# Scores and state sums of 128-token chunks in halves of 64 tokens, on quarters of the TensorE array

## Chip, cores, metric

The kernel runs on one core of a Trainium2 chip. The metric is the device time of one execution in microseconds (us); lower is better. A changed kernel is timed against the kernel before, and for this kernel a difference of 0.2% (2 us) is about what can be told from none.

## What is computed

Three layers follow each other: a gated linear attention and two feed-forward layers. Inputs are float32, but the weights come as float64 and are split on the chip into a high and a low part.

```python
# attention: 4 batches, 8 heads, 768 tokens, head size 48
for t in range(S):
    state = alpha[:, :, t, :, None] * state + np.einsum('bhd,bhe->bhde', k[:, :, t], v[:, :, t])
    y[:, :, t] = np.einsum('bhd,bhde->bhe', q[:, :, t], state)
x = y.transpose(0, 2, 1, 3).reshape(3072, 384)
x = ((x @ w_a) * (x @ w_b)) @ w_out                                   # 384 -> 1536 -> 384
h = x @ w_in                                                          # 384 -> 2048
return (np.maximum(h, 0.0) + alpha2 * np.minimum(h, 0.0)) @ w_out2    # 2048 -> 384
```

## The kernel before

The tokens are worked on in six blocks of 512: block n holds 128 consecutive tokens of each of the four batches. One batch's 128 tokens are a chunk, so a block is four chunks (`BC`), and there are 24. The state of a batch, `Z[:, c]`, passes from its chunk in one block to its chunk in the next. The eight heads lie as four pairs j, a pair's head i on partitions 64*i to 64*i+47.

A chunk (function `chunk`, from L353) does this. VectorE (DVE) forms the running products of alpha by two scans (L401, L411) and multiplies k and q by them (L416), so that inside the chunk plain matmuls do. TensorE (PE) transposes k (`pe_k`, tile kps, L452), and ScalarE (ACT) copies it out to `ks` (L456). PE forms the scores `A` of all 128 x 128 token pairs of each head (`pe_a`, L470: 48 rows deep, 128 columns out, 128 tokens streamed; the two heads of a pair in the two row halves of the array). DVE multiplies them by the causal mask into `As` (`ev_a`, L479). PE forms the chunk's own state sum `dS` from ks and v (`pe_d`, L503), and the result `y`: v against the masked scores (`intra`, L521, 128 rows deep) plus the old state against q (`inter`, L527, 48 by 48, four matmuls in the four quarters of the array at once). DVE then adds dS to Z (`kept`, L582), ACT and DVE split y into a high and a low part (L605, L609) for the feed-forward matmuls. All of these matmuls are float32; in the trace each leaves two MATMUL and two LDWEIGHTS records.

Block 0 starts from no state (`start`); block 1 (`moved`) packs its heads into 384 rows by three shift matmuls (`pe_m`, L563) and so does y in two parts; the last block (`end`) needs no dS.

The feed-forward layers are groups of nine matmuls of 128 x 512: `pa`, `pb` and `acc` of the first layer, `pi` and `acc` of the second (`mm3`, L641 to L644). Its DVE work is the product (L771) and the low part (L668).

The order on each engine is fixed when the program is built. A planner (`Graph.run`) gives every operation a duration (the numbers in `A("PE", 1200, ...)`), a key (its due time) and dependencies, and takes, engine by engine, the ready operation of the smallest key. A chunk's operations are due some 9.5 us apart ahead of their block, and lie between feed-forward groups. Where the planner leaves PE idle early in the program, `fill` puts matmuls on constants there (`wp`, L184), for 0.7 of the idle time. PSUM: the scores `A` and the result `y` use one tile of two banks in turn (tag `pair`, ring `pring`); kps and dS use a third bank in turn (tag `att`).

Of the kernel before, what the change touches and what calls it, by code (L numbers as in the profile page):

```python
# [21 lines left out]
P = 128  # L22
CH = 128
BC = 4
# [114 lines left out]
def body(tc, akq, v, vg, w_a, w_b, w_o1, w_in, w_o2, beta, out):  # L139
# [13 lines left out]
    with ExitStack() as ctx:  # L153
# [199 lines left out]
        def chunk(g):  # L353
# [118 lines left out]

            def ev_a(h):
                def f():
                    if 0 in h:
                        s["As"] = tp.tile([P, 2, NJ, CH], F32, name="As", tag="As", bufs=1)
                    m = mask.rearrange("p (o t) -> p o t", o=1).to_broadcast([P, len(h) * NJ, CH])
                    flat = lambda x: x.rearrange("p i j t -> p (i j) t")
                    nc.vector.tensor_tensor(out=flat(s["As"][:, h[0] : h[-1] + 1]),  # L479
                                            in0=s["A"][h[0]] if start else flat(s["A"]), in1=m, op=ALU.mult)  # L480
                return f

            w = sring.take()
            if start:
                (b0, w0, h0), (b1, w1, h1) = bank(1), bank(2)
                abanks = (b0, b1)
                pa = A("PE", 1200, pe_a, [k1, q1, *w0, *w1])
                a0 = A("DVE", 660, ev_a([0]), [pa, *w])
                a1 = A("DVE", 660, ev_a([1]), [pa, a0])
# [7 lines left out]
            if ks is not None:  # L497
                def pe_d():
                    s["dS"] = dbank("dS")[:, :, 0:D]
                    for j in range(NJ):  # L500
                        for i in range(2):
                            hs = slice(64 * i, 64 * i + 64)
                            nc.tensor.matmul(s["dS"][hs, j, :], s["ks"][:, j, hs],  # L503
                                             s["v"][:, 2 * j + i, 0:D], start=True, stop=True)
# [7 lines left out]

            def y_of(j, rows=slice(0, P)):
                return s["y"][rows, j % 2, j // 2, :]

            def intra(j, first, last):
                for i in range(2):
                    o = 64 * (i ^ (j & 1))  # L520
                    nc.tensor.matmul(y_of(j, slice(o, o + 64)), s["v"][:, 2 * j + i, :],  # L521
                                     s["As"][:, i, j, :], start=first, stop=last)

            def inter(j, last):
                for i in range(2):
                    ps, o = slice(64 * i, 64 * i + D), 64 * (i ^ (j & 1))
                    nc.tensor.matmul(y_of(j, slice(o, o + D)), Z[ps, c, j, :], qT()[ps, j, :],  # L527
                                     start=False, stop=last)

            def pe_y():  # L530
                s["y"] = two_banks("y")
                if start:

                    for j in range(KT):
                        intra(j, j < 2, False)
                    for j in range(KT):
                        for i in range(2):
                            nc.tensor.matmul(y_of(j, slice(64 * i, 64 * i + 64)), s["vg"][:, j, i, :],
                                             s["As"][:, i ^ (KT & 1), KT, :], start=False, stop=j > 0)
                    return  # L540
                if moved:
                    intra(KT, True, False)
                    inter(KT, True)
                    return
                for j in range(NJ):
                    intra(j, j < 2, False)
                for j in range(NJ):
                    inter(j, j > 1)

            py = A("PE", 1600 if start else 600 if moved else 1600, pe_y, [a0, a1, lv, q1, zs, *pring.take()])  # L550
            yhold = pring.last()
            if moved:
# [4 lines left out]
                def pe_m():  # L557
                    for j in range(KT):
                        intra(j, j < 2, False)
                    for j in range(KT):  # L560
                        inter(j, False)
                    for j in range(KT):
# [13 lines left out]
            if not end:  # L576
                def kept():
# [17 lines left out]
            def two(part):  # L595

                x = xt[n][:, part, :, cols].rearrange("p (k b) t -> p b k t", b=2)
                y = s["y"][:, :, 0 : NJ // 2, :]
                return [(x, y)] if nt == NJ else [(x[:, :, 0], y[:, :, 0]), (x[:, 0, 1], y[:, 0, 1])]
# [30 lines left out]

        for g in range(NG):
            chunk(g)
# [274 lines left out]
def layout(q, k, v, alpha, moe_w_a, moe_w_b, moe_w_out, moe2_w_in, moe2_w_out, moe2_alpha):  # L907
# [6 lines left out]
    def padded(x, fill):  # L914
# [14 lines left out]
    swap = lambda x, j: x[::-1] if j & 1 else x  # L929
    vg[..., D:] = (  # L930
        swap(v[:, H - 2 :, :CH].swapaxes(0, 1), KT).reshape(2, B, CH, KT, GR).transpose(1, 2, 3, 0, 4)
    )
# [3 lines left out]
        np.concatenate([np.arange(D) + (2 * t + i) * D, np.arange(GR) + (2 * KT + k) * D + GR * t])  # L936
        for t in range(KT) for i, k in zip(swap((0, 1), t), swap((0, 1), KT))
# [27 lines left out]
```

## Time and profile before

| what | us |
|---|---|
| timed runs | 976.03 to 976.87, median 976.53 |
| profiled execution: span from first to last instruction | 974.6 |
| its own time beside the span | not given; the median of the timed runs lies 1.9 above the span |
| PE busy | 962.7 (99%) |
| DVE busy | 607.0 (62%) |
| ACT busy | 252.3 (26%) |

The span is what the sums of the prediction are made against, and 1.9 us are added for the time around it. A PE that is shown busy is not a PE at its peak: the records overlap, and how long a piece of work holds PE is read from the starts of what follows.

### The profile page before, as it was taken

The page shows a single profiled execution, that of the slowest core. Times are in us where ns is not written, and L with a number is a line of the kernel's source. Part 1 is how long each engine was busy: PE and PEld are TensorE (multiplying, and loading weights), DVE is VectorE, ACT ScalarE, POOL GpSimd, SP SyncE. Part 2 cuts the span into 40 slices and gives each one's busy share as a digit, 9 for nine tenths or more (in the row PEclk, how much of TensorE's full clock was granted, in tenths as well). Part 3 has the DMA queues.
Part 4 walks back from the last instruction along what each step waited for, and adds up shares of the span by engine and source line. Part 5 has one row for each costly group of instructions (what it writes and reads, how often), then busy time and mean ns, then how long its engine had stood idle before and what let it go on. Part 6 is the DMA issues. An engine that isn't in the chain of part 4 may idle for free.

```text
span 974.6 us, 12831 instructions
## 1 busy us (share of the span) xinstructions
PE 962.7 (99%) x5330; PEld 777.9 (80%) x5330; DVE 607.0 (62%) x867; ACT 252.3 (26%) x417; POOL 4.5 (0%) x18
## 2 busy tenths in 40 slices
PE   6999999999999999999999999999999999999998
PEld 5777888778877887887788888888888888888886
DVE  8989888667678868876322254554555545545554
ACT  2444443232333333242121121111111111111111
POOL 1000000000000000000000000000000000000000
PEclk9999999999999999999999999999999999999999
DMA  8962000133457535652055550020100200200000
GB/s 324 405 245 76 1 12 1 55 119 126 170 197 233 199 119 203 193 199 99 33 186 201 193 192 22 1 98 1 65 33 1 86 11 1 98 1 1 32 1 33
DMA packets 31066, 103.92 MB, mean 107 GB/s; under 512 B 3488, under 2 KB 4256, under 8 KB 31008
## 3 DMA queue, kind: packets, MB, share of 16 engines
q1 hardware_dynamic: 30864, 102.97, 29.5%
q8 instruction: 42, 0.69, 0.3%
q10 hardware_dynamic: 144, 0.13, 0.0%
q14 instruction: 16, 0.13, 0.0%
HBM read 74.78 MB, written 26.74 MB: 104 GB/s over the span
## 4 chain that ended last, share of the span: by engine, by line
PE 99%; DVE 0%; DMA 0%; issue 0%; ACT 0%; DVEq 0%; ACTq 0%
PE acc L641 12%; PE acc L644 12%; PE acc L642 12%; PE pi L641 7%; PE pi L642 7%; PE pi L644 7%; PE pa L641 5%; PE pb L641 5%; PE pa L642 5%; PE pb L642 5%; PE pb L644 5%; PE pa L644 5%; PE A L470 3%; PE y L521 2%; PE y L527 1%; PE dS L503 1%
## 5 line engine op out<-in xcount | busy, mean ns | idle before, releaser
L664 ACT CAST gh<-ng 128x512 fp32r<-128x512 f32 x96 | 59.5, 620 | 327.8 <-DVE ng L877 271.2
L873 DVE TENSOR_SCALAR ng<-pi,betaT 128x512 f32<-128x512 f32 x96 | 72.1, 751 | 106.5 <-PE pi L644 105.5
L771 DVE TENSOR_TENSOR a_sb<-a_sb,pb 128x512 f32<-128x512 f32 x72 | 49.5, 688 | 108.4 <-PE pb L644 108.4
L668 DVE TENSOR_TENSOR gl<-ng,gh 128x512 fp32r<-128x512 f32 x96 | 66.3, 691 | 80.0 <-ACT gh L664 79.9
L641 PE MATMUL acc<-gh,v 128*128 128x512 f32 x288 | 113.4, 394 | 0.0
L641 PE MATMUL pi<-x,v 128*128 128x512 f32 x288 | 113.3, 393 | 0.0
L642 PE MATMUL pi<-x,v 128*128 128x512 f32 x288 | 112.7, 391 | 0.0
L644 PE MATMUL acc<-gl,v 128*128 128x512 f32 x288 | 112.7, 391 | 0.0
L642 PE MATMUL acc<-gh,v 128*128 128x512 f32 x288 | 112.0, 389 | 0.0
L641 PE MATMUL acc<-gh,wo 128*128 128x512 f32 x216 | 86.7, 401 | 0.0
L641 PE MATMUL pa<-x,wa 128*128 128x512 f32 x216 | 86.3, 400 | 0.0
L641 PE MATMUL pb<-x,wb 128*128 128x512 f32 x216 | 86.1, 399 | 0.0
L644 PE MATMUL acc<-gl,wo 128*128 128x512 f32 x216 | 84.8, 392 | 0.0
L642 PE MATMUL pa<-x,wa 128*128 128x512 f32 x216 | 84.6, 392 | 0.0
L642 PE MATMUL pb<-x,wb 128*128 128x512 f32 x216 | 84.6, 392 | 0.0
L642 PE MATMUL acc<-gh,wo 128*128 128x512 f32 x216 | 84.1, 390 | 0.0
L768 ACT COPY a_sb<-pa 128x512 f32<-128x512 f32 x72 | 42.3, 588 | 155.4 <-PE pa L644 155.4
L644 PE MATMUL pi<-x,v 128*128 128x512 f32 x288 | 81.6, 391 | 0.0
L664 ACT CAST gh<-a_sb 128x512 fp32r<-128x512 f32 x72 | 44.8, 622 | 126.7 <-DVE a_sb L771 120.8
L877 DVE SCALAR_TENSOR_TENSOR ng<-pi,ng 128x512 f32<-128x512 f32 x96 | 66.4, 691 | 3.1
L641 PEld LDWEIGHTS pi<-x,v 128*128 128x128 f32 x288 | 54.1, 188 | 13.7 <-DVE ng L877 2.1
L644 PEld LDWEIGHTS acc<-gl,v 128*128 128x128 f32 x288 | 54.1, 188 | 12.6
(109 smaller groups left out, 1430.8 us busy)
## 6 DMA issues: line engine op xcount, KB each, us to landing
kq<-in_akq SPq DMA_DIRECT2D x24, 512.0 KB, 4.5
w2d<-ws SPq DMA_DIRECT2D x16, 768.0 KB, 3.7
v<-w2d SPq DMA_DIRECT2D x16, 768.0 KB, 5.5
x2d<-x SPq DMA_DIRECT2D x18, 512.0 KB, 3.7
x<-x2d SPq DMA_DIRECT2D x6, 1536.0 KB, 6.9
ra<-in_akq SPq DMA_DIRECT2D x24, 258.5 KB, 3.4
v<-in_v SPq DMA_DIRECT2D x24, 256.0 KB, 4.9
rs<-in_w_in SPq DMA_DIRECT2D x8, 768.0 KB, 6.0
```

The lines of the kernel that those rows point to most:

```text
L470: nc.tensor.matmul(A[i][:, j, :], kT()[ps, j, :], qT()[ps, j, :], start=True, stop=True)
L503: nc.tensor.matmul(s["dS"][hs, j, :], s["ks"][:, j, hs], s["v"][:, 2 * j + i, 0:D], start=True, stop=True)
L521: nc.tensor.matmul(y_of(j, slice(o, o + 64)), s["v"][:, 2 * j + i, :], s["As"][:, i, j, :], start=first, stop=last)
L641: nc.tensor.matmul(o, lh, rh, start=first and n == 0, stop=False)
L642: nc.tensor.matmul(o, ll, rh, start=False, stop=False)
L644: nc.tensor.matmul(o, lh, rl, start=False, stop=last and n == len(pairs) - 1)
L664: nc.scalar.copy(gq[idx][0], src())
L668: nc.vector.tensor_tensor(out=gl, in0=src(), in1=gh.bitcast(F32), op=ALU.subtract)
L768: nc.scalar.copy(b["a"], ba["t"])
L771: nc.vector.tensor_tensor(out=b["a"], in0=b["a"], in1=bb["t"], op=ALU.mult)
L873: nc.vector.tensor_scalar(out=b["n"], in0=bh["t"], scalar1=0.0, scalar2=betaT[:, i : i + 1], op0=ALU.min, op1=ALU.mult)
L877: nc.vector.scalar_tensor_tensor(out=b["n"], in0=bh["t"], scalar=0.0, in1=b["n"], op0=ALU.max, op1=ALU.add)
```

## The change

In all blocks but the first, a chunk's 128 tokens are taken as two halves h of 64. Scores are formed only inside a half (`A` is 64 by 64, 16 matmuls for 8, in the four quarters of the array), and the mask is 64 by 64 for both halves, so DVE's masking has 512 elements a partition for 1024. What the first half gives to the second goes by the state: the state sum is formed for each half (16 matmuls for 8, 64 rows deep), a new DVE operation `mid` adds the first half's sum to Z and gives `z1`, and the second half's `inter` uses z1. `pe_d` and `pe_y` become `pe_cross` (half of the intra matmuls, and both state sums) and, behind `mid`, `pe_own` (the other half of intra, and inter in 16 matmuls for 8). dS no longer has a bank of its own in these blocks: it lies in the free part of y's two banks, which are therefore also held until `mid` and `kept` have read them. The last block now transposes k too and forms the first half's sum. In block 1 the y of the shifted heads is no longer made in two parts: `pe_m` holds the three shift matmuls alone. Once, ACT copies a quarter of the mask (`halve`). The heads take other slots in y, and the rows of w_a and w_b are permuted to suit when the inputs are laid out. Block 0 keeps its matmuls.

```diff
--- before.py
+++ after.py
...
-            if not end:
+            if not (start and end):
                 def pe_k():
...
             def pe_a():
-                s["A"] = [b(f"A{i}") for i, b in enumerate(abanks)] if start else two_banks("A")
-                A = s["A"] if start else [s["A"][:, i] for i in range(2)]
+                if start:
+                    s["A"] = [b(f"A{i}") for i, b in enumerate(abanks)]
+                    for j in range(NJ):
+                        for i in range(2):
+                            ps = slice(64 * i, 64 * i + D)
+                            nc.tensor.matmul(s["A"][i][:, j, :], kT()[ps, j, :], qT()[ps, j, :],
+                                             start=True, stop=True)
+                    return
+                s["A"] = two_banks("A").rearrange("p i j t -> p i (j t)")[:, :, 0 : NJ * HC]
+                A = s["A"].rearrange("p i (j t) -> p i j t", t=HC)
                 for j in range(NJ):
-                    for i in range(2):
-                        ps = slice(64 * i, 64 * i + D)
-                        nc.tensor.matmul(A[i][:, j, :], kT()[ps, j, :], qT()[ps, j, :],
-                                         start=True, stop=True)
-
-            def ev_a(h):
+                    for h in range(2):
+                        hs = slice(h * HC, (h + 1) * HC)
+                        for i in range(2):
+                            ps = slice(64 * i, 64 * i + D)
+                            nc.tensor.matmul(A[hs, i, j, :], kT()[ps, j, hs], qT()[ps, j, hs],
+                                             start=True, stop=True)
+
...
+                    m = mask[:, 0:HC].rearrange("p (a o t) -> p a o t", a=1, o=1).to_broadcast([P, 2, NJ, HC])
+                    a = s["A"].rearrange("p i (j t) -> p i j t", t=HC)
+                    nc.vector.tensor_tensor(out=s["As"], in0=a, in1=m, op=ALU.mult)
...
-                pa = A("PE", 1200, pe_a, [k1, q1, *pring.take()])
-                a0 = a1 = A("DVE", 1200, ev_a([0, 1]), [pa, *w], 0, slack)
+                pa = A("PE", 600, pe_a, [k1, q1, *pring.take()])
+                a0 = a1 = A("DVE", 700, ev_a(0), [pa, halved[0], *w], 0, slack)
...
+            def slot_of_head(j, i):
+                return 2 * i + j // 2, j % 2
+
+            def y_of(k, rows=slice(0, P), t=slice(0, CH)):
+                return s["y"][rows, k // 2, k % 2, t]
...
-            py = A("PE", 1600 if start else 600 if moved else 1600, pe_y, [a0, a1, lv, q1, zs, *pring.take()])
...
+                part_of = lambda h: slice(h * HC, (h + 1) * HC)
+                def intra(j, i, h, first):
+                    k, p = slot_of_head(j, i)
+                    nc.tensor.matmul(y_of(k, half(p), part_of(h)), s["v"][part_of(h), 2 * j + i, :],
+                                     s["As"][part_of(h), i, j, :], start=first, stop=False,
+                                     skip_group_check=True)
+                def inter(j, i, h, z, last):
+                    k, p = slot_of_head(j, i)
+                    ps = slice(64 * i, 64 * i + D)
+                    nc.tensor.matmul(y_of(k, slice(64 * p, 64 * p + D), part_of(h)), z[ps, j, :],
+                                     qT()[ps, j, part_of(h)], start=False, stop=last,
+                                     skip_group_check=True)
+                def pe_cross():
+                    s["y"] = two_banks("y")
+                    flat = s["y"].rearrange("p i j t -> p i (j t)")
+                    s["dS"] = [flat[:, 1 - h, 2 * CH : 2 * CH + NJ * D].rearrange("p (j d) -> p j d", d=D)
+                               for h in range(2)]
+                    for j in range(NJ):
+                        for h in range(2):
+                            intra(j, 1 - h, h, j < 2)
+                    for j in range(NJ):
                         for i in range(2):
+                            for h in range(1 if end else 2):
+                                nc.tensor.matmul(s["dS"][h][half(i), j, :], s["ks"][part_of(h), j, half(i)],
+                                                 s["v"][part_of(h), 2 * j + i, 0:D], start=False,
+                                                 stop=j == NJ - 1, skip_group_check=True)
+                def mid():
+                    s["z1"] = s["At"][:, NJ * CH : NJ * CH + NJ * D].rearrange("p (j d) -> p j d", d=D)
+                    nc.vector.tensor_tensor(out=s["z1"], in0=s["dS"][0], in1=Z[:, c, :, :], op=ALU.add)
+                def pe_own():
+                    for j in range(NJ):
+                        for i in range(2):
+                            intra(j, i, i, False)
+                    for h, z in ((0, Z[:, c]), (1, s["z1"])):
+                        for j in range(NJ):
+                            for i in range(2):
+                                inter(j, i, h, z, h == 1 and j > 1)
+                pc = A("PE", 850, pe_cross, [a0, ks, lv, *pring.take()])
+                yhold = pring.last()
+                kring.use(pc)
+                z1 = A("DVE", 360, mid, [pc, zs])
+                py = A("PE", 850, pe_own, [z1, zs, q1])
+                yhold.append(z1)
...
                 def pe_m():
-                    for j in range(KT):
-                        intra(j, j < 2, False)
-                    for j in range(KT):
-                        inter(j, False)
-                    for j in range(KT):
-                        nc.tensor.matmul(y_of(j), shift[:, j, :], s["y3"], start=False, stop=j > 0)
-
+                    for k in range(KT):
+                        nc.tensor.matmul(y_of(k), shift[:, k, :], s["y3"], start=False, stop=k > 0,
+                                         skip_group_check=True)
+
+                lhold.append(py)
                 x = A("ACT", 280, ev_3, [py, *yring.take()])
-                py = A("PE", 2200, pe_m, [x])
+                py = A("PE", 750, pe_m, [x])
...
-                        nc.vector.tensor_tensor(out=z, in0=s["dS"], in1=z, op=ALU.add)
-
-                x = A("ACT" if start else "DVE", 360, kept, [ds] if start else [ds, zs, py])
-                dhold.append(x)
+                        nc.vector.tensor_tensor(out=z, in0=s["dS"][1], in1=s["z1"], op=ALU.add)
+
+                x = A("ACT" if start else "DVE", 360, kept, [ds] if start else [z1, py])
+                (dhold if start else yhold).append(x)
+                if not start:
+                    sring.use(x)
...
+                def halve():
+                    nc.scalar.copy(mask[HC:, 0:HC], mask[HC:, HC:])
+                halved.append(G.add("ACT", 250, halve, block_at[1] - 60000, masked))
...
```

The planner lays the engines' orders out anew. On PE, around the fourth chunk of block 2, these rows stand before (a row is a line, an operation, out<-in and its shape; pa is a feed-forward group):

```order
L452 MATMUL kps<-plus,kq 128x128 x4
L470 MATMUL A<-kq 128x128 x8
L503 MATMUL dS<-v,ks 64x48 x8
L641 MATMUL pa<-x,wa_1500 128x512
L642 MATMUL pa<-x,wa_1500 128x512
L641 MATMUL pa<-x,wa_1500 128x512
L642 MATMUL pa<-x,wa_1500 128x512
L641 MATMUL pa<-x,wa_1500 128x512
L642 MATMUL pa<-x,wa_1500 128x512
L644 MATMUL pa<-x,wa_1500 128x512 x3
L521 MATMUL y<-As,v 64x128 x8
L527 MATMUL y<-kq,Z 48x128 x8
```

After the change the same chunk's `pe_cross` (first two rows) and `pe_own` (last three rows; `y<-kq,As` is the inter on z1, which lies in As's tile) stand like this, and its A stands two groups earlier, by itself:

```order
L558 MATMUL y<-As,v 64x64 x8
L581 MATMUL y<-v,ks 64x48 x16
L699 MATMUL pb<-x,wb_1747 128x512
L700 MATMUL pb<-x,wb_1747 128x512
L699 MATMUL pb<-x,wb_1747 128x512
L700 MATMUL pb<-x,wb_1747 128x512
L699 MATMUL pb<-x,wb_1747 128x512
L700 MATMUL pb<-x,wb_1747 128x512
L702 MATMUL pb<-x,wb_1747 128x512 x3
L558 MATMUL y<-As,v 64x64 x8
L565 MATMUL y<-kq,Z 48x64 x8
L565 MATMUL y<-kq,As 48x64 x8
```

What moved: the attention interrupts the feed-forward groups three times for this chunk (A, cross, own) instead of twice, with one group of nine between cross and own; so it is in all 16 chunks of blocks 2 to 5, but for block 2's first, where two groups stand there.

On DVE the rows around that chunk's `mid` (L587) are, after the change:

```order
L829 TENSOR_TENSOR a_sb<-a_sb,pb 128x512
L496 TENSOR_TENSOR As<-A,mask 128x512
L791 TENSOR_TENSOR x_2336<-part_1169,x_2336 128x512
L726 TENSOR_TENSOR gl<-a_sb,gh 128x512
L417 TENSOR_TENSOR kq<-kq,ra 128x1024
L587 TENSOR_TENSOR As<-y,Z 128x192
L408 RECIPROCAL invs<-ra 128x4
L431 TENSOR_TENSOR Z<-Z,ra 128x192
L412 SCALAR_TENSOR_TENSOR ra<-ra,invs 128x516
L829 TENSOR_TENSOR a_sb<-a_sb,pb 128x512
L632 TENSOR_TENSOR Z<-y,As 128x192
```

Before, a chunk's y waited for no sum of its dS on DVE; now `pe_own` waits for `mid`, which stands behind the next chunk's product of k and q (L417) here, and `kept` (L632) follows behind the next product of the feed-forward. In the whole order there are 125 `wp` matmuls where there were 84; all 41 new ones lie among block 1's chunks.

## Rows read from the trace of the kernel before

**Rows 1.** The page, its first line.

```profile
span 974.6 us, 12831 instructions
```

**Rows 2.** Busy time by engine (x records) in three stretches: block 1's chunks, feed-forward only, block 2's chunks.

```profile
core 0: us, PE busy (x) PEld busy (x) DVE busy (x) ACT busy (x) POOL busy (x), PEclk, DMA share, GB/s
36.00:48.00 12.00, 12.00 (x85) 8.61 (x81) 10.94 (x19) 4.96 (x11) 0.00 (x0) 1.00 1.03 411
100.00:170.00 70.00, 70.00 (x307) 57.45 (x306) 61.98 (x87) 30.71 (x45) 0.00 (x0) 1.00 0.02 5
170.00:225.00 55.00, 55.00 (x439) 43.36 (x439) 38.63 (x56) 13.49 (x23) 0.00 (x0) 1.00 0.34 109
```

**Rows 3.** Timeline of PE (start, length, line, out<-in, records), block 2's first chunk.

```profile
175.09 0.60 PE L452 MATMUL kps<-plus,kq 128*128 128x128 f32 x4
...
176.71 0.50 PE L641 MATMUL pb<-x,wb 128*128 128x512 f32 x1
177.05 0.40 PE L642 MATMUL pb<-x,wb 128*128 128x512 f32 x1
...
178.21 0.85 PE L644 MATMUL pb<-x,wb 128*128 128x512 f32 x3
...
179.93 0.40 PE L642 MATMUL acc<-gh,wo 128*128 128x512 f32 x1
```

**Rows 4.** Timeline of PE, block 3's second chunk.

```profile
278.48 0.60 PE L452 MATMUL kps<-plus,kq 128*128 128x128 f32 x4
279.01 1.16 PE L470 MATMUL A<-kq 48*128 48x128 f32 x16
...
281.05 0.39 PE L642 MATMUL acc<-gh,wo 128*128 128x512 f32 x1
...
282.66 0.39 PE L644 MATMUL acc<-gl,wo 128*128 128x512 f32 x1
282.98 1.09 PE L521 MATMUL y<-As,v 128*64 128x128 f32 x16
284.01 0.65 PE L527 MATMUL y<-kq,Z 48*48 48x128 f32 x16
...
284.93 0.40 PE L642 MATMUL pa<-x,wa 128*128 128x512 f32 x1
```

**Rows 5.** Records begun by a stretch's end (x), block 2's first chunk: A, dS, inter.

```profile
175.61:175.85 0.24, 0.23 (x4) 1.00 0.00 0
175.61:176.51 0.90, 0.89 (x16) 1.00 0.00 0
...
178.98:179.11 0.13, 0.12 (x4) 1.00 0.00 0
178.98:179.46 0.48, 0.47 (x16) 1.00 0.00 0
...
182.88:182.92 0.04, 0.03 (x4) 1.00 0.00 0
182.88:183.07 0.19, 0.18 (x8) 1.00 0.00 0
182.88:183.30 0.42, 0.41 (x16) 1.00 0.00 0
```

**Rows 6.** Groups of DVE instructions by line and shape: busy us, mean ns.

```profile
L416 DVE TENSOR_TENSOR kq<-kq,ra 128x1024 f32<-128x1024 f32 x24 | 29.3, 1219 | 3.3 <-DMA kq<-in_akq 3.3
L479 DVE TENSOR_TENSOR As<-A,mask 128x1024 f32<-128x1024 f32 x20 | 24.5, 1223 | 12.2 <-PE A L470 12.2
L582 DVE TENSOR_TENSOR Z<-dS,Z 128x192 f32<-128x192 f32 x16 | 5.7, 354 | 4.6 <-PE y L527 4.6
L479 DVE TENSOR_TENSOR As<-A,mask 128x512 f32<-128x512 f32 x8 | 5.5, 684 | 0.4 <-PE A L470 0.4
```

**Rows 7.** Timeline of DVE: the mask behind the scores of block 2's first chunk.

```profile
176.83 1.23 DVE L479 TENSOR_TENSOR As<-A,mask 128x1024 f32<-128x1024 f32 x1 [0.19 <-PE A L470]
```

**Rows 8.** Timeline of PE in block 1's second chunk: filling matmuls and what follows.

```profile
52.99 1.27 PE L184 MATMUL wp<-ones 128*128 128x256 bf16 x10
54.09 0.49 PE L307 MATMUL cl<-c,plus 128*128 128x384 f32 x1
```

More of the change, by code (lines that the diff above doesn't have):

```diff
@@ L23 @@
 CH = 128
+HC = CH // 2
 BC = 4
@@ new lines, in ev_a @@
+            def ev_a(i):
+                def f():
+                    if i == 0:
+                        s["At"] = tp.tile([P, 2 * NJ * CH], F32, name="As", tag="As", bufs=1)
+                        w = CH if start else HC
+                        s["As"] = s["At"][:, 0 : 2 * NJ * w].rearrange("p (i j t) -> p i j t", i=2, j=NJ)
+                    if start:
+                        m = mask.rearrange("p (o t) -> p o t", o=1).to_broadcast([P, NJ, CH])
+                        nc.vector.tensor_tensor(out=s["As"][:, i], in0=s["A"][i], in1=m, op=ALU.mult)
+                        return
+                    m = mask[:, 0:HC].rearrange("p (a o t) -> p a o t", a=1, o=1).to_broadcast([P, 2, NJ, HC])
+                    a = s["A"].rearrange("p i (j t) -> p i j t", t=HC)
+                    nc.vector.tensor_tensor(out=s["As"], in0=a, in1=m, op=ALU.mult)
@@ L487, in chunk @@
                 pa = A("PE", 1200, pe_a, [k1, q1, *w0, *w1])
-                a0 = A("DVE", 660, ev_a([0]), [pa, *w])
-                a1 = A("DVE", 660, ev_a([1]), [pa, a0])
+                a0 = A("DVE", 660, ev_a(0), [pa, *w])
+                a1 = A("DVE", 660, ev_a(1), [pa, a0])
+                masked.append(a1)
                 h0.append(a0)
@@ L492, in chunk, with half @@
             else:
-                pa = A("PE", 1200, pe_a, [k1, q1, *pring.take()])
-                a0 = a1 = A("DVE", 1200, ev_a([0, 1]), [pa, *w], 0, slack)
+                pa = A("PE", 600, pe_a, [k1, q1, *pring.take()])
+                a0 = a1 = A("DVE", 700, ev_a(0), [pa, halved[0], *w], 0, slack)
                 pring.use(a0)
-            if ks is not None:
+            def slot_of_head(j, i):
+                return 2 * i + j // 2, j % 2
+            def y_of(k, rows=slice(0, P), t=slice(0, CH)):
+                return s["y"][rows, k // 2, k % 2, t]
+            def half(p):
+                return slice(64 * p, 64 * p + 64)
+            if start:
                 def pe_d():
@@ L511, in chunk @@
                 vring.use(ds)
[L515 to L528, printed above, removed]
@@ L550, in chunk, with pe_y @@
-            py = A("PE", 1600 if start else 600 if moved else 1600, pe_y, [a0, a1, lv, q1, zs, *pring.take()])
-            yhold = pring.last()
+                def pe_y():
+                    s["y"] = two_banks("y")
+                    for i in range(2):
+                        for j in range(NJ):
+                            k, p = slot_of_head(j, i)
+                            if k < KT:
+                                nc.tensor.matmul(y_of(k, half(p)), s["v"][:, 2 * j + i, :], s["As"][:, i, j, :],
+                                                 start=j < 2, stop=False)
+                    for k in range(KT):
+                        for p in range(2):
+                            nc.tensor.matmul(y_of(k, half(p)), s["vg"][:, k, p, :],
+                                             s["As"][:, KT // 2, 2 * (KT % 2) + p, :], start=False, stop=k > 0)
@@ L557, in pe_m @@
                 def pe_m():
[L558 to L563 removed]
+                    for k in range(KT):
+                        nc.tensor.matmul(y_of(k), shift[:, k, :], s["y3"], start=False, stop=k > 0,
+                                         skip_group_check=True)
+                lhold.append(py)
                 x = A("ACT", 280, ev_3, [py, *yring.take()])
[L566 removed]
+                py = A("PE", 750, pe_m, [x])
                 yring.use(py)
@@ L928, in layout @@
     KT, GR = H * D // P, 64 - D
[L929 to L932, printed above, removed]
+    head = lambda k, p: 4 * (k % 2) + 2 * p + k // 2
+    for p in range(2):
+        vg[:, :, :, p, D:] = v[:, head(KT, p), :CH].reshape(B, CH, KT, GR)
     rows = np.concatenate([
-        np.concatenate([np.arange(D) + (2 * t + i) * D, np.arange(GR) + (2 * KT + k) * D + GR * t])
-        for t in range(KT) for i, k in zip(swap((0, 1), t), swap((0, 1), KT))
+        np.concatenate([np.arange(D) + head(t, p) * D, np.arange(GR) + head(KT, p) * D + GR * t])
+        for t in range(KT) for p in range(2)
     ])
```

36 lines of the change are left out of this document (12 added, 24 removed).

## The prediction

> **What bounds the kernel.** I read the span first, then busy time by stretch, then the timeline of PE at single chunks. The span is 974.6 us [rows 1]. PE is busy for all of every stretch from block 1's chunks on, at a granted clock of 1.00 (the upper level, 2.4 GHz), while DVE has 10.94 of 12 us in block 1's chunks, but only 38.63 of 55 in block 2's [rows 2]. A busy PE may still be waiting inside its records, so I measured the holding time from starts. With feed-forward alone 307 records take 70.00 us, 0.228 us each [rows 2]. I then counted each visit of the attention between feed-forward groups as the time from the end of the last feed-forward slot to the second feed-forward start behind it, less one slot of 0.228; so it holds the cost of changing over. A stall for another engine would show as a visit longer than its steps and its changing over; below these account for all of it, so from block 2 on I take PE to run one thing after another without a wait. What PE no longer does there comes off the time; what DVE no longer does is worth nothing by itself.
>
> **What a visit costs now.** Kps and A of block 2's first chunk hold PE from 175.09 to 177.05 less 0.23: 1.73 us. Its dS, alone, runs from the end of the three records at 178.21 (178.89) to 179.93 less 0.23: 0.81 [rows 3]. The commoner chunk makes two visits: kps, A and dS from 278.48 to 281.05 less 0.23, 2.34; y from 282.66 plus 0.23 to 284.93 less 0.23, 1.81 [rows 4]. That is 4.15 a chunk. In block 5, which has neither kps nor dS, I estimate A at 1.73 less four transposes of 128 columns at 0.11, 1.29, and with y 3.10.
>
> **How fast the steps go.** A's records start in twos, the two row halves together: from the 4th to the 16th record 0.66 us go by, six steps of 0.11, with 128 columns streamed. dS's start in twos as well, with 48 columns streamed and 64 columns of weights: six steps in 0.35, 0.058 each. Inter's start in fours, one for each quarter, all four within 0.04 us, and each later step of 128 columns takes about 0.11 again [rows 5]. So quarters do run side by side, and the time of a step goes by columns. No row shows four quarters with 64 columns. Half of inter's step gives 0.055; dS's step, the nearest with 64 columns of weights, gives 0.058. I take 0.058. The other bound is that a step of four keeps inter's 0.11, since no row has records coming faster on average than four in 0.11.
>
> **The change on PE, per chunk of blocks 2 to 4.**
> - A: 16 matmuls are 32 records, in fours eight steps of 0.058 for eight of 0.11: 0.42 less. Kps with A: 1.31.
> - Cross: four steps of intra and eight of dS (twice the records, in fours) where dS alone had eight: 0.81 + 4 x 0.058 = 1.04.
> - Own: from y's 1.81. Intra's remaining half is four steps of 0.058 for eight of 0.11: 0.65 less. Inter has twice the records at half the columns: eight steps of 0.058 for four of 0.11, 0.02 more. Going over from intra to inter now costs something: intra holds PE for 1.03 (282.98 to 284.01 [rows 4]) where eight steps make 0.88, and inter's first step takes 0.15 instead of 0.11 [rows 5]. Of these 0.19, one start of 0.05 stays as in any visit; 0.14 goes, since both are quarters now. Own: 1.04.
> - Sum 3.39 for 4.15: 0.76 less, although there are three visits for two. Times 12: 9.1 us less. (Block 2's first chunk made three visits, so saves more; those of blocks 3 and 4 had dS beside y and save less. I let these cancel.)
>
> **Block 5.** Kps is new, and cross holds one state sum: four steps of intra and four of dS, 0.81 as dS had. 1.31 + 0.81 + 1.04 = 3.16 for 3.10, four times: 0.2 more.
>
> **Block 1.** Each chunk saves at least the same 0.76 (3.0 in all). But the planner puts 41 more filling matmuls between these chunks; ten hold PE from 52.99 to 54.09 [rows 8], 0.11 each, so 4.5 us. They stand where the planner sees PE idle, since the way from scores to split is longer by one trip to DVE while the feed-forward of block 1 can't begin before the last split; and DVE, at 10.94 of 12, paces this stretch. DVE gains little. The mask of 1024 elements takes 1223 ns and the one of 512 elements 684, and `mid` is a second sum like `kept`, 354 [rows 6]: 0.19 less a chunk. I take block 1 as unchanged. The bounds are 3.0 less (the fill covers only what was idle) and 1.5 more (4.5 less 3.0, if PE paces it).
>
> **The new wait.** Own waits for `mid`, `mid` for cross. What hides it is the group of nine between them: 9 x 0.228 = 2.05 us. DVE took up the scores' mask at 176.83 [rows 7], 0.12 after PE had gone on at 176.71 [rows 3]. Taking 0.12 each way, one long operation in front (the product of k and q, 1219 ns) and 354 for `mid` [rows 6], that is 1.8 us: hidden, with 0.2 to spare. Behind a `mid` that waits on DVE stand the next chunk's scans and the feed-forward's product, whose users come a group or more later. Without the group PE would wait 0.6 to 1.8 a chunk. The mask's copy is one ACT operation long before, and ACT, like the four added copies of ks in block 5, has room (13.49 of 55 [rows 2]). Loads are unchanged.
>
> **Sum.** -9.1 + 0.2 + 0 = -8.9: a span of 965.7 for 974.6. The median of the timed runs lies 1.9 above the span; I keep that: 967.6. Its own range, with block 1's bounds and steps between 0.055 and 0.066, is 963 to 972.
>
> **Rivals.**
> - Small quarters don't pay (the other side). The chunks of blocks 2 to 5 hold 12 x 32 + 4 x 28 = 496 steps of four. If a step takes inter's 0.11 whatever its columns, because records or weights can't come faster, 496 x 0.052 = 25.8 us come on top: 993.4. It decides from a step of 0.076 on (8.9 / 496 = 0.018 more). For it: no row shows a higher average rate. Against it: inside a step four records start within 0.04, and dS's steps shrink with its columns and weights. Chance 0.13.
> - The Trainium skill's page "TensorE: Matmul & The Clock Gate", section "Wait — 56ns, not 53.3ns?", holds that starts of matmuls come no closer than about 25 ns however few columns they stream; by that a step of four would be 0.10, and the sum would come to about 988 (an estimate from that page). In inter records start closer than that inside a step, but its average of 0.11 for four does not contradict the page.
> - `mid` comes late. If two products stand in front of it rather than one, 0.12 + 2.44 + 0.35 + 0.12 - 2.05 = 1.0 us is lost; in half of the 16 chunks that is 7.8: 975.4. It turns the sign from 0.56 a chunk on. For it: DVE is in order, and an operation in front may itself wait for PE. Against it: in the rows around block 2's fourth chunk only one product and shorter operations stand there, none of which needs the group behind cross. Chance 0.05.
> - PE isn't what paces: the gain is taken by other waits and the time stays within 2 us. Rows 2 speak against it. Chance 0.03.
> - Block 1 shortens as well by its 3 to 4 us: 963 to 964. Chance 0.06.
>
> **Numbers.** The forecast has 0.73. About 0.2% (2 us) is what a measurement of this kernel can tell from no change. Faster by more: 0.73 + 0.06 = 0.79. Within it: the late `mid` and the absorbed gain, 0.08. Slower: 0.13. The range 963 to 976 holds all but the slow rival and the edge below, some 0.85.
>
> **What would show it.** Right: A's records start in fours some 0.06 apart, cross and own hold PE for about 1.04 each, and PE goes from the group before own into own without a gap. Wrong: steps of four near 0.11 (then A gains nothing and the sums double), an idle PE that waits for L587, or a stretch of block 1 that is longer than before by more than 2 us.

## The result and the profile after

The changed kernel takes 966.72 us (median, 966.1 to 966.85) where the kernel before takes 976.7 in the same comparison: a ratio of 0.9896, 95% interval 0.9882 to 0.991. That is 10.0 us less; forecast were 8.9.

The page of the changed kernel gives the span [rows 1], and PE is as full as before:

```profile
span 965.2 us, 15549 instructions
PE 952.7 (99%) x6667; PEld 770.4 (80%) x6667; DVE 600.4 (62%) x887; ACT 253.9 (26%) x422; POOL 4.4 (0%) x18
```

Busy time in the three stretches of [rows 2]. PE is busy throughout, and between 170 and 225 us it begins 711 records where it began 439:

```profile
core 0: us, PE busy (x) PEld busy (x) DVE busy (x) ACT busy (x) POOL busy (x), PEclk, DMA share, GB/s
36.00:48.00 12.00, 12.00 (x144) 9.16 (x143) 10.64 (x18) 5.74 (x12) 0.00 (x0) 1.00 1.03 411
100.00:170.00 70.00, 70.00 (x308) 57.43 (x307) 61.68 (x89) 28.94 (x43) 0.00 (x0) 1.00 0.03 8
170.00:225.00 55.00, 55.00 (x711) 43.24 (x710) 36.84 (x59) 14.56 (x25) 0.00 (x0) 1.00 0.38 120
```

The timeline of PE at block 2's first chunk answers to [rows 3]:

```profile
173.08 0.85 PE L702 MATMUL pa<-x,wa 128*128 128x512 f32 x3
173.77 0.60 PE L453 MATMUL kps<-plus,kq 128*128 128x128 f32 x4
174.30 0.69 PE L481 MATMUL A<-kq 48*64 48x64 f32 x32
174.92 0.50 PE L699 MATMUL pb<-x,wb 128*128 128x512 f32 x1
175.26 0.39 PE L700 MATMUL pb<-x,wb 128*128 128x512 f32 x1
...
176.42 0.85 PE L702 MATMUL pb<-x,wb 128*128 128x512 f32 x3
177.20 0.46 PE L558 MATMUL y<-As,v 64*64 64x64 f32 x16
177.48 0.63 PE L581 MATMUL y<-v,ks 64*64 64x48 f32 x32
178.04 0.51 PE L699 MATMUL acc<-gh,wo 128*128 128x512 f32 x1
178.39 0.40 PE L700 MATMUL acc<-gh,wo 128*128 128x512 f32 x1
...
181.60 0.85 PE L702 MATMUL pa<-x,wa 128*128 128x512 f32 x3
182.39 0.46 PE L558 MATMUL y<-As,v 64*64 64x64 f32 x16
182.67 0.41 PE L565 MATMUL y<-kq,Z 48*48 48x64 f32 x16
182.89 0.40 PE L565 MATMUL y<-kq,As 48*48 48x64 f32 x16
183.23 0.51 PE L699 MATMUL pb<-x,wb 128*128 128x512 f32 x1
183.57 0.40 PE L700 MATMUL pb<-x,wb 128*128 128x512 f32 x1
```

Read as the prediction read [rows 3, 4] (three records end 0.68 after they start, and the second feed-forward start less 0.23 ends a visit): kps and A hold PE for 175.26 - 0.23 - 173.76 = 1.27 us, cross for 178.39 - 0.23 - 177.10 = 1.06, own for 183.57 - 0.23 - 182.28 = 1.06. Over the 16 chunks of blocks 2 to 5 cross and own are 1.04 to 1.06 each. Kps and A are one visit of 1.27 or 1.28 in six of them; in most of the others A stands alone (0.83, once 0.91), and kps alone (0.45) or right behind an own, which it lengthens by 0.38.

Records of A begun by a stretch's end (x), for [rows 5]: four in the first 0.03 us, then 24 more between 0.13 and 0.48, six steps of 0.058.

```profile
174.30:174.33 0.03, 0.03 (x4) 1.00 0.00 0
174.30:174.43 0.13, 0.13 (x8) 1.00 0.00 0
174.30:174.78 0.48, 0.48 (x32) 1.00 0.00 0
```

The groups of DVE for [rows 6]: the mask takes 686 ns, `mid` 356.

```profile
L496 DVE TENSOR_TENSOR As<-A,mask 128x512 f32<-128x512 f32 x20 | 13.7, 686 | 5.1 <-PE A L481 5.1
L587 DVE TENSOR_TENSOR As<-y,Z 128x192 f32<-128x192 f32 x20 | 7.1, 356 | 10.2 <-PE y L581 9.8
```

**Where the time came from.** From the first feed-forward matmul to the 109th of `pa`, which lies behind all of block 1's chunks, PE takes 99.28 us for 99.67; from there to the 541st of `pa`, which is block 5's first and lies behind all chunks, 354.99 for 363.33; from there to PE's last start 470.81 for 470.80. So 8.3 us come from blocks 2 to 5 and 0.4 from block 1. Of the rest of the span's 9.4, the first feed-forward matmul starts 0.9 earlier, and 0.2 go back behind PE's last. That start differs by 1.1 us among the variants below that have the same work ahead of it, so I don't count these as an effect.

### The profile page after: what moved, and what is told of

The parts are those of the page before. It is cut to its first block, busy times and chain, and to the rows that moved or that the text cites. A ratio compares the mean times of both kernels' runs of the same rounds, so it can differ in the third digit from the quotient of the medians.

```text
span 965.2 us, 15549 instructions
## 1 busy us (share of the span) xinstructions
PE 952.7 (99%) x6667; PEld 770.4 (80%) x6667; DVE 600.4 (62%) x887; ACT 253.9 (26%) x422; POOL 4.4 (0%) x18
## 4 chain that ended last, share of the span: by engine, by line
PE 99%; DVE 0%; DMA 0%; ACT 0%; issue 0%; DVEq 0%; ACTq 0%
PE acc L699 12%; PE acc L702 12%; PE acc L700 12%; PE pi L699 7%; PE pi L702 7%; PE pi L700 7%; PE pb L699 5%; PE pa L699 5%; PE pa L700 5%; PE pb L700 5%; PE pb L702 5%; PE pa L702 5%; PE wp L185 2%; PE y L558 2%; PE kps L453 1%; PE A L481 1%
## 5 line engine op out<-in xcount | busy, mean ns | idle before, releaser
L699 PEld LDWEIGHTS acc<-gh,v 128*128 128x128 f32 x288 | 54.0, 188 | 12.3
```

The lines of the kernel that those rows point to most:

```text
L699: nc.tensor.matmul(o, lh, rh, start=first and n == 0, stop=False)
```

## The experiments

All are edits of the changed kernel. Their reference is its 966.7; the kernel before stood at 976.5, 976.0 and 976.4 in the three sets.

**scores_as_before: the row halves again, in all blocks.**

```diff
-                for j in range(NJ): for h in range(2): for i in range(2):
-                    nc.tensor.matmul(A[hs, i, j, :], kT()[ps, j, hs], qT()[ps, j, hs], ...)
+                for j in range(NJ): for i in range(2):
+                    nc.tensor.matmul(s["A"][:, i, j, :], kT()[ps, j, :], qT()[ps, j, :], ...)
```

(shortened; the mask is taken from the two diagonal quarters, in two operations of 64 partitions. The planner is told 1200 ns for A, for 600, and 1400 for the mask, for 700, and lays out the order anew.)

> The scores alone go back to row halves (8 matmuls of 128 columns for 16 of 64); DVE masks the two diagonal blocks in two operations of 64 partitions, some 0.68 us each. If the gain is PE's shorter steps, an A visit grows by 8 x (0.11 - 0.058) = 0.42 us, 16 to 20 times: 966.7 + 6.7 to 8.4 = 973.4 to 975.1. If the gain came from somewhere else than A's steps (another order, fewer changes of mode), the time stays within 2 us of 966.7.

Measured: 993.79 us (993.35 to 995.22), ratio to the kernel before 1.0182 (1.0167 to 1.0197). That is 27 us more than the changed kernel, so neither expectation held. The visits grew as the first had it: A alone 1.30, kps with A 1.73 to 1.74, 0.47 more a chunk and 9.3 in all 20. The rest is not in the visits. The waits of PE (us in total, times, longest):

```profile
PE pa L699 <- DMA x<-x: 7.6, 5, 3.0
```

They stand in the first 6 us of the feed-forward of blocks 2 and 3, which wait for the moves of `x` behind the block's last split. The mean granted clock is 0.991 over a span of 992.3 for 0.999, worth at most 0.008 x 992.3 = 7.9 us, since some of the time at the lower clock is these waits themselves. 9.3 + 7.6 + 7.9 = 24.8, so at least 2.3 of the 27.1 us by which the span grew stay open. A chunk that takes longer breaks something at the block's start, and this run isn't the price of A's steps. Nor does it tell A's steps from the second operation on DVE, which lengthens the same way.

**mask_twice: DVE multiplies by the mask twice.**

```diff
-                    nc.vector.tensor_tensor(out=s["As"], in0=a, in1=m, op=ALU.mult)
+                    for _ in range(2):
+                        nc.vector.tensor_tensor(out=s["As"], in0=a, in1=m, op=ALU.mult)
```

(The planner is told 1360 ns for the mask, for 700, so the order changes too; this holds for the two runs below that double the mask in some blocks as well.)

> Every masking in blocks 1 to 5 is done twice on DVE (0.68 us more a chunk, as long as before), nothing else changes. If PE bounds blocks 2 to 5, nothing moves there and block 1, where DVE is nearly full, grows by at most 4 x 0.68 = 2.7 us: 966.7 to 969.4. If DVE's shorter mask is where the gain came from, the time goes back to about 976.

Measured: 974.9 us (974.08 to 976.34), ratio 0.9985 (0.9975 to 0.9994). It is slower by 8.2 us, near the second expectation's 976, but not by DVE's work in the chunks: the visits between feed-forward groups are those of the changed kernel. 1.1 us are lost in block 1, 7.1 between the 109th and the 541st `pa`, most of them where block 2's feed-forward begins. I call the stretch from a block's last own to the block's first `pa` the hand-over to that block.

**inter_in_32s: inter in pieces of 32 tokens, twice the matmuls.**

```diff
-                    nc.tensor.matmul(y_of(k, ..., part_of(h)), z[ps, j, :], qT()[ps, j, part_of(h)], ...)
+                    ts = slice(h * HC + u * 32, h * HC + u * 32 + 32)
+                    nc.tensor.matmul(y_of(k, ..., ts), z[ps, j, :], qT()[ps, j, ts], ...)
```

(shortened)

> The matmuls of inter stream 32 tokens instead of 64, twice as many, same result. It asks what ends a step of four quarters. If the columns streamed alone, a step falls to 0.03 us and own stays at 1.05: 966.7. If the 48 columns of weights or the rate of records end it at 0.04 to 0.056, own grows by 0.2 to 0.45 us: 970 to 975.7. If the rival of the prediction held in a weaker form (four records need some 0.10), own would grow by 1.1 us: 985 or more.

Measured: 972.66 us (971.51 to 974.85), ratio 0.9965 (0.9951 to 0.9979). The second expectation held: own holds PE for 1.31, 0.26 more. Sixteen steps of four take 0.045 each for eight of 0.056, so half the columns make a step only a fifth shorter. Something other than the 32 streamed columns ends it; the 48 columns of weights and the rate of records are not told apart here. From the 109th to the 541st `pa` that is 4.2 us, 16 chunks by 0.26. Most of the rest of the profiled run is one wait in block 1, in the middle of cross's 32 records:

```profile
52.46 0.50 PE L582 MATMUL y<-v,ks 64*64 64x48 f32 x21
56.02 0.43 PE L582 MATMUL y<-v,ks 64*64 64x48 f32 x11 [3.06 <-issue]
```

In the stretch from 52.5 to 54 us the DMA queues show one packet of instructions, while loads fill the engines:

```profile
q1 hardware_dynamic: 113, 0.62, 100.4%
q8 instruction: 1, 0.02, 4.3%
```

From 45 to 52.5 and from 54 to 56.02 there is none. I read it as PE waiting for its own instructions, but that isn't shown: no run takes the loads away, and the changed kernel has such a packet between 53.5 and 54 and no wait of PE. The profiled run is the slowest of the five (974.85; two others took 972.2 and 971.51), so the wait need not be in each of them.

**no_fill_block1: 78 of the filling matmuls left out** (all those among block 1's chunks, not only the 41 that the change added).

```diff
+            fills.append(t0)
+            if len(fills) > 4:
+                return
             mpool.log.append([])
```

> The 78 filling matmuls behind block 0's (8.5 us of PE) are left out; they add nothing to the result. If they only cover what PE would wait for anyway, as the prediction had it, the time stays at 966.7 within 1 us. If PE paces block 1, up to 8.5 us go. If the fills keep the clock up, the granted clock falls in block 1's stretch and the time grows.

Measured: 965.7 us (964.67 to 967.26), ratio 0.9893 (0.9879 to 0.9908): the same as with them. From the first feed-forward matmul to the 109th `pa` it takes 98.74 us for 99.28. But these 0.5 us less are the sum of two effects, since the third expectation's clock came too. PE now waits in block 1, the last time for ACT's x behind the last chunk's y, and behind that the granted clock is at the lower level (1.2 GHz). A row of PE's timeline and a stretch:

```profile
87.69 0.80 PE L704 MATMUL pa<-x,wa 128*128 128x512 f32 x1 [1.39 <-ACT x L662]
87.40:90.60 3.20, 2.91 (x7) 2.33 (x8) 3.20 (x6) 2.15 (x4) 0.00 (x0) 0.51 0.28 105
```

That costs 2.91 x 0.49 = 1.4 us, so at full clock the fills left out would give some 2 us. The timed runs agree: the two with a mean granted clock of 1.00 took 964.67 and 964.81, the other two 966.59 (the profiled one, 0.998) and 967.26 (0.996). So the fills cover idle time all but some 2 us, and in two runs of four the clock took that back.

**mask_twice_block2 and mask_twice_late: the same doubling in block 2 alone, and in blocks 3 to 5 alone** (`range(2 if n == 2 else 1)` and `range(2 if n >= 3 else 1)`).

> The mask of the scores is done twice on DVE in block 2's four chunks alone (0.68 us a chunk more on DVE, on the way from a chunk's scores to its split). Doing it twice in blocks 1 to 5 had cost 8.2 us (974.9), of which I read some 1.4 in block 1's own chunks. Theory of the hand-over: the rest is lost where block 2's feed-forward waits for the last chunk's split and moves, so block 2's masks alone cost nearly all of it: 971.5 to 974. Rival, that DVE's load costs everywhere alike: 4 of 16 chunks, 968 to 969. Second rival, that the chunk of block 3 which the planner puts into that gap is what is late: no change, 966.4 to 967.4.

> The mask of the scores is done twice on DVE in blocks 3 to 5 alone (12 chunks, 8.2 us of DVE work). Theory of the hand-over to block 2: these chunks lie between feed-forward groups with time to spare, so 966.4 to 968. Rival, that DVE's load costs everywhere alike: 12 of the 20 chunks that the earlier run doubled, about 971.5. Second rival, that block 3's first chunk, which fills the gap before block 2's feed-forward, is what is late: 971 to 974.

Measured: block 2 alone 969.46 us (968.23 to 970.7), ratio 0.9931 (0.9918 to 0.9943); blocks 3 to 5 alone 972.74 (972.02 to 973.72), ratio 0.9967 (0.9954 to 0.9979). That is 2.7 and 6.0 us, together about what the run before lost. The hand-over to block 2 alone, my theory, can't be it. The times lie close to the rival of DVE's load (968 to 969 and 971.5), and the later run's also in the second rival's range (971 to 974), that the next block's first chunk, put into the gap before a block's feed-forward, is late. The traces bear out that second rival. In the first kernel PE waits at the hand-over to block 2 for block 3's first chunk, for its mask and, 1.42 us more at 230.47, for its `mid`:

```profile
228.14 0.46 PE L559 MATMUL y<-As,v 64*64 64x64 f32 x16 [1.34 <-DVE As L497]
```

That chunk's mask is not doubled (one operation of 0.68 us at 227.40), so it is its place in the order that costs. The second kernel has its waits at the next hand-over, to block 3. Timeline of PE:

```profile
311.27 0.40 PE L566 MATMUL y<-kq,As 48*48 48x64 f32 x16
...
313.56 0.39 PE L703 MATMUL acc<-gl,wo 128*128 128x512 f32 x1
313.79 0.60 PE L453 MATMUL kps<-plus,kq 128*128 128x128 f32 x4
314.31 0.69 PE L481 MATMUL A<-kq 48*64 48x64 f32 x32
318.40 0.71 PE L559 MATMUL y<-As,v 64*64 64x64 f32 x16 [3.39 <-issue]
318.86 1.08 PE L582 MATMUL y<-v,ks 64*64 64x48 f32 x32
320.62 0.70 PE L559 MATMUL y<-As,v 64*64 64x64 f32 x16 [0.69 <-DVE As L588]
...
322.88 0.77 PE L700 MATMUL pa<-x,wa 128*128 128x512 f32 x1
```

The row at 311.27 ends block 3's last own. Nine feed-forward matmuls are left before block 3's own first `pa`, so the planner puts in block 4's whole first chunk, whose mask and `mid` PE now waits for. (The profile puts the 3.39 down to `issue`; on DVE the doubled mask runs from 316.89 to 318.30, behind other work.) Behind the wait the granted clock is at the lower level (1.2 GHz):

```profile
318.40:324.50 6.10, 5.41 (x104) 4.81 (x105) 6.10 (x10) 2.49 (x4) 0.00 (x0) 0.51 0.96 305
```

3.39 + 0.69 of waits and 5.41 x 0.49 = 2.65 of slow clock are 6.7 us; the span grew by 5.9.

This can be counted in the order of the program for every kernel: how many feed-forward matmuls stand between the last own (or y) of a block and the block's first `pa`. The waits are those of the profiled runs, of 0.2 us and more. The two kernels that are not in the table have the changed kernel's numbers and no wait there.

| kernel | block 2 | 3 | 4 | 5 | PE waits at hand-overs, us | time |
|---|---|---|---|---|---|---|
| before | 54 | 45 | 45 | 45 | none | 976.7 |
| changed | 27 | 36 | 36 | 45 | none | 966.72 |
| scores_as_before | 9 | 9 | 36 | 36 | 7.6 | 993.79 |
| mask_twice | 9 | 18 | 27 | 36 | 2.1 + 1.4 | 974.9 |
| mask_twice_block2 | 9 | 36 | 45 | 45 | 1.3 + 1.4 | 969.46 |
| mask_twice_late | 27 | 9 | 27 | 36 | 3.4 + 0.7 | 972.74 |
| scores_as_before_45 | 27 | 36 | 18 | 36 | 0.8 | 971.36 |
| last_block_whole | 27 | 36 | 27 | 45 | 2.4 | 968.81 |
| mask_twice_late_early | 27 | 45 | 36 | 45 | none | 966.63 |
| last_block_whole_early | 27 | 36 | 45 | 45 | none | 965.86 |
| early | 27 | 36 | 45 | 45 | none | 966.09 |
| no_group_between | 36 | 45 | 45 | 45 | none | 972.28 |

**scores_as_before_45: A's row halves in blocks 4 and 5 alone** (the edit of scores_as_before under `if n >= 4`).

> Blocks 4 and 5 alone form their scores as before, all 128 x 128 pairs in the two row halves of the array (the mask is taken from the two diagonal quarters, so the result is the same). A's steps by the trace: eight of 0.11 for eight of 0.058 a chunk, 0.42 to 0.45 us, and 8 chunks: 970.0 to 970.5 if PE is what paces there and the 27 us of the earlier run came from the hand-overs to blocks 2 and 3. Rival, that PE's steps there are covered by something else: 966.7. Second rival, that the longer chunk also breaks the hand-over to blocks 4 and 5: 974 and more, with PE waiting for the move of x at a block's start.

Measured: 971.36 us (970.78 to 972.12), ratio 0.9951 (0.9939 to 0.9964). A alone takes 1.30 for 0.83, kps with A 1.74 for 1.27: 8 x 0.47 = 3.7 us, the price of A's steps (expected 3.4 to 3.6). The waits for the moves of `x` at the hand-over to block 4, with 18 matmuls left, add 0.8; the span grew by 4.4. The first expectation was right in the price, the third in its place but not in its size.

**last_block_whole: block 5 as before the change** (A of whole chunks, the mask of 1024, y in one visit, no kps; one DVE operation sets the mask's corner back).

> Block 5 alone works as before the change: scores of whole chunks in row halves, a mask of 1024 elements, y in one visit, no transposed k and no state sum; one DVE operation sets the mask's corner back. By the trace block 5's visits go from 1.27 + 1.05 + 1.05 to about 1.30 + 1.81 us a chunk, 0.26 less, four times 1.0: 965.7. If the visits of block 5 cost what the prediction took (1.31 + 0.81 + 1.04): 966.7 to 966.5. If block 5's own way helps at the end of the program in another way, the time rises: 967 and more.

Measured: 968.81 us (968.27 to 970.58), ratio 0.9928 (0.9914 to 0.9941): slower, in the third expectation's range, though block 5's visits came down as expected (1.30 + 1.81 a chunk). The timeline of PE at the hand-over to block 4:

```profile
394.68 0.40 PE L597 MATMUL y<-kq,As 48*48 48x64 f32 x16
...
401.42 1.16 PE L471 MATMUL A<-kq 48*128 48x128 f32 x16
404.98 0.47 PE L736 MATMUL pa<-x,wa 128*128 128x512 f32 x1 [2.40 <-DMA x<-x]
```

Behind it 3.40 us at the lower clock level:

```profile
405.80:409.20 3.40, 3.40 (x9) 2.63 (x8) 2.88 (x5) 0.60 (x2) 0.00 (x0) 0.50 1.01 386
```

And SP's queue, start and length of an issue: the six moves come behind a load of 768 KB.

```profile
395.57 1.29 SPq L234 DMA_DIRECT2D rs<-in_w_o  x1
397.28 3.94 SPq L709 DMA_DIRECT2D x<-x  x6
```

Their issue alone takes 3.94 us, and in the stretch from 390 to 410 they land 6.3 after issue (median). So 27 matmuls, 6.2 us, and A's 1.3 don't do here, while mask_twice and mask_twice_late have 27 there and no wait. I put it down to the load ahead of the moves, which no run takes away. In the changed kernel 27 do at the hand-over to block 2, with two kps and A beside them, barely: the last of the six moves lands at 228.14 and the first `pa` starts at 228.15 (before, at 227.13 and 229.13). Busy times of the changed kernel around it, 0.1 us of PE missing:

```profile
225.00:265.00 40.00, 39.90 (x252) 32.51 (x251) 29.88 (x44) 14.68 (x23) 0.00 (x0) 1.00 0.41 146
```

**mask_twice_late_early, last_block_whole_early and early: due times.** The planner takes the chunks of blocks 3 to 5 as due earlier, by 6 us in the first and by 3 us in the other two:

```diff
-            key = block_at[n] - (BC - c) * 9500 - 6000 if n else c * 1000 - 100000
+            key = block_at[n] - (BC - c) * 9500 - 6000 - (0, 0, 0, 6000, 6000, 6000)[n] if n else c * 1000 - 100000
```

> The mask done twice in blocks 3 to 5 again (972.74 us when the planner's due times were left as they were; there no feed-forward matmul lay between the last result y of block 3 and block 3's first feed-forward matmul), but the planner takes the chunks of blocks 3 to 5 as due 6 us earlier, by which 45, 36 and 45 matmuls lie there. Theory that the loss was the wait at the hand-over alone: 966 to 968, with no wait of PE at any block's start, though DVE does the 8.2 us more. Rival, that DVE's load itself costs: it stays at 971 to 973.

(The y that I had counted from in mask_twice_late was that of block 4's first chunk. From block 3's own last y nine matmuls lay there, as the table has it.)

> Block 5 whole as before the change, and the chunks of blocks 3 to 5 due 3 us earlier (45 feed-forward matmuls before block 4's first one for 27). Theory: the 2.5 us and the cold clock behind them at the hand-over to block 4 go, and block 5's 1.0 us shows: 965.3 to 966, 1 us under the kernel with early chunks alone. Rival, that block 5's way before costs by itself: it stays at 968 to 969.

> The changed kernel with the chunks of blocks 3 to 5 due 3 us earlier and nothing else (27, 36, 45 and 45 matmuls between the last y and the first feed-forward matmul of blocks 2 to 5, for 27, 36, 36 and 45). There was no wait at those hand-overs to take away, so by the theory nothing changes: 966 to 967.

Measured: mask_twice_late_early 966.63 us (966.31 to 967.35), ratio 0.9903 (0.9888 to 0.9918); last_block_whole_early 965.86 (965.62 to 965.99), ratio 0.9894 (0.988 to 0.9907); early 966.09 (965.93 to 966.61), ratio 0.9897 (0.9884 to 0.9911). The doubled masks, 8.2 us of DVE's time, cost nothing once the order leaves room: 6.1 us come back, and the only wait of PE that is left is that at the program's start:

```profile
PE kps L453 <- DVE kq L417: 8.0, 1, 8.0
```

With early due times block 5's old way no longer loses: its visits are 12.45 us for 13.36, and its median is 0.2 us under early alone. Whether it gains the 0.9 of the visits is within the intervals. No version is clearly faster than the changed kernel: the lowest medians, 965.7 (no_fill_block1) and 965.86, are 1.0 and 0.9 under it.

**no_group_between: cross, mid and own in one piece.**

```diff
-                pc = A("PE", 850, pe_cross, [a0, ks, lv, *pring.take()])
-                z1 = A("DVE", 360, mid, [pc, zs])
-                py = A("PE", 850, pe_own, [z1, zs, q1])
+                def all_three():
+                    pe_cross(); mid(); pe_own()
+                py = z1 = A("PE", 1700, all_three, [a0, ks, lv, zs, q1, *pring.take()])
```

(shortened; `mid` is still DVE's, but the planner gives it no time of its own.)

> Cross, mid and own follow each other in one piece on PE, so that no group of nine hides mid. By the prediction PE then waits 0.6 to 1.8 us a chunk at own, and saves the changing over of one visit, 0.3 to 0.4: 16 chunks behind block 1, so +4 to +23 us, 971 to 990, with a wait of PE for z1 in every chunk. Rival, that mid is so quick that nothing is lost, or that the shorter way of a chunk gains as much at the hand-overs: 966 to 967.

Measured: 972.28 us (971.34 to 973.56), ratio 0.9961 (0.9949 to 0.9974). The timeline of PE in a chunk of block 4:

```profile
356.71 0.63 PE L581 MATMUL y<-v,ks 64*64 64x48 f32 x32
357.83 0.46 PE L558 MATMUL y<-As,v 64*64 64x64 f32 x16 [0.48 <-DVE As L587]
```

And PE's waits for `mid`, in total, times, longest:

```profile
PE y L558 <- DVE As L587: 9.5, 20, 0.5
```

The joined visit takes 2.44 us for 1.05 + 1.05: 0.34 more, 5.4 in 16 chunks, of the 5.6 measured. (In the profiled run block 1 takes 1.1 more as well, and the first feed-forward matmul starts 0.8 earlier.) `mid` without its cover costs PE 0.48, under the 0.6 to 1.8 expected: nothing stood in front of it on DVE, which idles 28.3 us ahead of its 20 `mid`.

## Why the prediction was right

- **Steps of four.** Taken as 0.058 between 0.055 and 0.11; measured 0.058 for A, intra and the state sums, 0.056 for inter. So the slow rival (0.11, 993.4 us) falls. The Trainium skill's page "TensorE: Matmul & The Clock Gate", section "Wait — 56ns, not 53.3ns?", has starts no closer than about 25 ns. A's records start 0.015 us apart on average (24 in 0.35 us), so here the measurement decides.
- **Blocks 2 to 4.** Forecast 1.31 + 1.04 + 1.04; measured 1.27, 1.05 and 1.05 where kps and A are one visit. The sum of all their visits is 49.74 before and 40.45 after, 9.3 less; forecast 9.1. scores_as_before_45 shows A's part by itself: 0.47 a chunk where the prediction had 0.42.
- **Block 5.** Forecast 0.2 more; measured 13.41 for 12.44, 1.0 more. The mis-sized term is cross: I took four steps for its one state sum, but its records start in twos, since only one half's rows are used, so there are eight steps as for two sums. It holds PE for 1.05, not 0.81; 4 x 0.24 = 1.0.
- **Block 1.** Taken as unchanged between -3.0 and +1.5; 0.4 less. By no_fill_block1 block 1's fills, old and new, fill idle time, all but some 2 us at full clock; without them the clock fell in two runs of four. What the 41 new ones cost by themselves no run shows.
- **The new wait.** `mid` ends 1.5 to 2.3 us before own starts in each of the chunks of blocks 2 to 5, so the group hides it with more room than the 0.2 that I gave it; and if it didn't, it would cost 0.3 to 0.5 a chunk, not 0.6 to 1.8, as long as DVE is free for it. The rival of the late `mid` falls.
- **Sum.** -9.3 + 1.0 - 0.4 = -8.7 beside the forecast's -8.9, and 0.7 from the program's start and end, which no part of the sum explains. That the two sums lie 0.2 apart is in part luck: block 5 was taken 0.8 too low, blocks 2 to 4 and block 1 together 0.6 too high.
- **What the prediction didn't see.** It costed waits inside a chunk, not the hand-over at a block's start. There the last y had 54, 45, 45 and 45 matmuls ahead of the block's first `pa`, and the last own has 27, 36, 36 and 45; with cross and own in one piece it has 36, 45, 45 and 45, so the third visit takes all that is lost at blocks 3 and 4 and a third of it at block 2. At block 2 the 27 just suffice. Every run with a 9 lost time there; of the two places with 18 one cost 0.8 and one 0.15 (mask_twice, block 3); one of the three with 27 at block 4 cost 2.4. In all, waits of 0.8 to 7.6 us a run, and what the lower clock took behind most of the long ones. So the count tells where to look, and not by itself what is lost. The forecast stood because the planner's order fell on the right side, which was luck: nothing in its sum said so. That the room at the hand-over, and not DVE's load, decides is shown by mask_twice_late_early for blocks 3 to 5.

## What to carry to other kernels

Where PE is full, price an edit by the holding time of each visit, steps by steps; count the steps by which quarters can truly run together (one half of a pair fills only two). Then look at where a chain of work ends against a deadline, here the first feed-forward group of a block: count in the order what stands between the last producer and the first user, before and after, and compare it with the trip of the data (PE, ACT, DVE, the DMA moves and what is queued ahead of them). A loss there can come twice, as the wait and as the lower clock behind it, and a shift of the due times can give it back.

## What the runs showed of the hardware

- Four records in the four quarters start within 0.02 us, and such steps follow each other every 0.056 to 0.058 us with 64 columns, every 0.045 with 32 columns and weights of 48. With records in two quarters only, the steps take 0.058 as well (the one state sum of block 5).
- A wait of PE of 2.40 us at block 4's start (last_block_whole) was followed by 3.40 us at a granted clock of 0.50, one of 3.39 at block 3's (mask_twice_late) by 6.10 at 0.51, and one of 1.39 in block 1 (no_fill_block1), 2.3 us behind one of 0.78, by 3.20 at 0.51. The wait of 3.06 in block 1 (inter_in_32s) was followed by none: the clock stayed at 1.00 from 52 to 62 us. The two waits of 1.34 and 1.42 at block 2's hand-over (mask_twice_block2) were followed by none either: it stayed at 1.00 from 226 to 236.
- In block 1, with the DMA engines full of loads, PE stood still once for 3.1 us in the middle of a run of small matmuls (inter_in_32s), with a packet of instructions on the queue at that time; the cause stays open.
